# Left sides of seven-product matrix multiplication read from weights already split in DRAM, and the last product's rows apart

## The chip, the core and the metric

One Trainium2 chip, one of its NeuronCores. The metric is device time in microseconds for one execution of the whole program, shown as the median of several runs. Engines are called as in the profile: PE (TensorE), DVE (VectorE), ACT (ScalarE), POOL (GpSimd) and SP (SyncE, which issues all DMAs here).

## What is computed

A chunked attention gives 3072 rows of 512, and two feed-forward networks (FFN) follow, all in float32:

```python
x = attn_out.transpose(0, 2, 1, 3).reshape(B * S, H * D)   # 3072 x 512
h = np.maximum(x @ w_in, 0.0)                              # 512 x 2048
x = h * h @ w_out                                          # 2048 x 512
g = x @ w_gate                                             # 512 x 1536
silu = g * (1.0 / (1.0 + np.exp(-g)))
out = silu * (x @ w_val) @ w_out2                          # 1536 x 512
```

## The kernel before, in words

**Precision.** Each float32 operand is split into a high part (`hi`, ACT: a conversion, L445) and a low part (`lo`, DVE or POOL: operand minus hi, L452). A product is three matmuls: lo x hi, hi x lo, hi x hi (`TERMS`).

**Stages.** The rows come in six blocks of 512, in three pairs. Attention runs beside the first blocks. The first FFN of blocks 0 to 3 goes directly (`first_layer`, `first_out`), to about 446 us. What is left goes by pairs with a recursion of seven products in place of eight (Winograd's form of Strassen's): the second FFN of pairs 0, 1 and 2, and the first FFN of pair 2. TensorE then runs `second_quads` and `out_layer` for pair 0 (446 to about 632 us), for pair 1 (to about 797), `first_quads` and `out_layer` for pair 2's first FFN, and its second FFN (to 1128.7).

**Left and right sides.** Each of the seven products has a left side, made from four quarters of a weight, and a right side, made from the pair's data. `sides` makes the left ones: `ax` and `ay` are two tiles of 512 columns, each half of which is a quarter. Its `part` splits a result into hi and lo in one of four slots: slot 0 is `ax` as it is (products 1 and 2), slot 1 is a sum (5), slot 2 what two differences leave in `ax` (6 and 3), slot 3 a difference (7) and the second half of `ay` as it is (4). They are written to DRAM (`keep_in`, `keep_out`) and read back for the product (`load_in`, `load_out`). There are 18 calls of `sides` for the second FFN's weights (`left2`, DRAM names `tma`, `tmb`) and 16 for the first's (`left1`, `tla`, `tlb`). The first FFN's weights were split for the direct stage already; `keep1` writes these hi and lo to DRAM (`w1d`, names `win` and `wout`) in two rounds of the direct stage, and for `left1` `whole_of` reads hi and lo back and adds them (L883), so that `sides` can work on whole weights. Right sides are made by `rights` (sums and differences L464, then splits).

**Evictions.** When a product is done in its PSUM bank, ACT copies it (products 1, 5, 6 in `second_quads`; L473) or DVE combines it (3, 2, 7, 4; L464); then TensorE may write the bank again.

**Order.** Nothing of the order is written by hand. The kernel first lists operations with estimated costs, due times (`SIDES`: `left1`'s sides are due from 560 every 16 of its time units) and buffers; `Plan.run` plays through them and fixes each engine's order, buffers, and which engine takes an operation that may go on two (a split's low part, a quarter-wide sum: DVE or POOL; relu-square: ACT or DVE). So a removed operation can move everything behind it. PE may take an operation out of turn, up to 8 ahead, if one before it isn't ready (`ahead=8`). The engines follow the order and wait by semaphores.

**The end.** In the last `out_layer` product 4 adds six groups into two banks (`bank[i][0]`, `bank[i][1]`, rows of the result), six matmuls a group; then both are copied and written out.

## Time and profile before

| | |
|---|---|
| time, median of 3 runs | 1133.24 us (1132.12 to 1135.54) |
| the profiled execution, its own time | 1134.11 us |
| its span (first to last instruction) | 1132.4 us |
| mean granted TensorE clock | 0.997 of full speed |
| PE busy | 97% |
| DVE / ACT / POOL busy | 79% / 54% / 18% |
| DMA moved | 322.02 MB, mean 284 GB/s |

A row of the profile names the line of the kernel, the engine, the operation and the tiles (out<-in, buffer numbers left out): `ps` is a PSUM bank, `r`, `x`, `xx` and `w` hold split operands, `u`, `a` and `t` data tiles, `f`, `ff`, `g`, `gg` the tiles of the sides. "Idle before" is the time in which the engine stood still ahead of the instruction, and the releaser is what ended it. A busy PE isn't PE at its peak, since the profile models matmul ends.

### The profile page before, as it was taken

To read this page: it belongs to the slowest core of one execution; us is meant where nothing else is said; L and a number is where in the kernel's file an instruction comes from. 1 tells how busy PE (TensorE), PEld (TensorE's weight loads), DVE (VectorE), ACT (ScalarE), POOL (GpSimd) and SP (SyncE) were. 2 spreads that over 40 slices of the span, in tenths; PEclk is the share of its full clock that TensorE was granted. 3 is DMA by queue.
4 is the path that set the end of the run, shared out by engine and by line. 5 is a ranking of instruction groups with operands and counts; after the bars stand their busy time and mean duration, and the time that the engine had idled before them with its cause. 6 is when DMAs were issued, how large, how long until landed. Compare 5 with 4: busy or idle time off the path is not lost.

```text
span 1132.4 us, 17301 instructions
## 1 busy us (share of the span) xinstructions
PE 1097.3 (97%) x6044; PEld 893.7 (79%) x6044; DVE 891.4 (79%) x1576; ACT 611.8 (54%) x1077; POOL 200.6 (18%) x157
## 2 busy tenths in 40 slices
PE   5899999999999999999999999989999999999998
PEld 4677788888788887888788788868888887888886
DVE  6999889868888998678999866899867864534981
ACT  3878745454456566555664444555657642433550
POOL 2231011312112343000613300335101000000000
PEclk9999999999999999999999999999999999999999
DMA  8756667878888878999799999989996677765562
GB/s 335 242 201 214 217 232 276 286 274 313 286 313 273 279 265 319 407 326 348 238 351 369 406 413 385 358 319 373 370 379 222 194 236 289 237 196 177 180 183 93
DMA packets 118503, 322.02 MB, mean 284 GB/s; under 512 B 12816, under 2 KB 25104, under 8 KB 118416
## 3 DMA queue, kind: packets, MB, share of 16 engines
q1 hardware_dynamic: 118416, 320.92, 79.8%
q8 instruction: 48, 0.79, 0.3%
q14 instruction: 39, 0.32, 0.1%
HBM read 227.02 MB, written 93.85 MB: 283 GB/s over the span
## 4 chain that ended last, share of the span: by engine, by line
PE 80%; DVE 9%; DMA 5%; ACT 3%; issue 2%; POOL 1%; SPq 0%; DVEq 0%; ACTq 0%; POOLq 0%
PE ps L942 34%; PE ps L1077 18%; PE ps L712 13%; PE ps L740 12%; PE ps L519 2%; PE ps L646 2%; DVE r L452 2%; DVE f L425 1%; DVE f L433 1%; DVE f L410 1%; DMA s<-in_k 1%; ACT r L445 1%; DMA tla<-g 1%; DMA u<-yd 1%; DVE u L464 1%
## 5 line engine op out<-in xcount | busy, mean ns | idle before, releaser
L942 PE MATMUL ps<-r,r 128*128 128x512 f32 x1353 | 325.3, 392 | 8.8 <-DVE a L464 4.5
L942 PEld LDWEIGHTS ps<-r,r 128*128 128x128 f32 x1353 | 254.8, 189 | 64.5 <-DVE a L464 5.0
L473 ACT ACTIVATE t<-ps 128x512 f32<-128x512 f32 x172 | 101.4, 594 | 191.3 <-PE ps L942 79.3
L1077 PE MATMUL ps<-r,r 128*128 128x512 f32 x774 | 182.5, 390 | 0.1
L1077 PEld LDWEIGHTS ps<-r,r 128*128 128x128 f32 x774 | 145.4, 188 | 30.8 <-DVE f L464 0.7
L740 PE MATMUL ps<-r,w 128*128 128x512 f32 x564 | 138.6, 396 | 2.8 <-DVE w L452 2.7
L740 PEld LDWEIGHTS ps<-r,w 128*128 128x128 f32 x564 | 105.3, 188 | 28.0 <-DVE w L452 4.7
L445 ACT ACTIVATE r<-u 128x512 fp32r<-128x512 f32 x144 | 85.6, 624 | 40.3 <-PE ps L1077 16.6
L452 DVE TENSOR_TENSOR r<-u,r 128x512 fp32r<-128x512 f32 x130 | 90.7, 716 | 17.0 <-ACT r L445 12.4
L712 PE MATMUL ps<-xx,r 128*128 128x512 f32 x384 | 96.9, 401 | 3.0 <-DVE r L452 2.5
L712 PE MATMUL ps<-x,r 128*128 128x512 f32 x384 | 94.3, 394 | 0.0
L712 PEld LDWEIGHTS ps<-xx,r 128*128 128x128 f32 x384 | 70.6, 188 | 22.2 <-DVE r L452 5.1
L464 DVE TENSOR_TENSOR t<-t,ps 128x512 f32<-128x512 f32 x72 | 49.1, 685 | 43.5 <-PE ps L942 39.7
L712 PEld LDWEIGHTS ps<-x,r 128*128 128x128 f32 x384 | 70.9, 188 | 15.4
L595 DVE STREAM_TRANSPOSE a<-t 32x128 f32<-32x128 f32 x256 | 77.4, 302 | 4.5 <-PE ps L646 0.2
L473 ACT ACTIVATE t<-t 128x512 f32<-128x512 f32 x72 | 45.5, 632 | 63.0 <-DVE t L464 60.3
L445 ACT ACTIVATE r<-a 128x512 fp32r<-128x512 f32 x63 | 39.1, 626 | 53.0 <-PE ps L1077 27.1
L452 POOL TENSOR_TENSOR r<-t,r 128x512 fp32r<-128x512 f32 x30 | 45.7, 1522 | 109.3 <-ACT r L445 91.2
L942 PE MATMUL ps<-x,r 128*128 128x512 f32 x231 | 62.3, 391 | 0.2 <-DVE x L452 0.2
L942 PE MATMUL ps<-r,x 128*128 128x512 f32 x243 | 61.0, 392 | 0.0
L452 POOL TENSOR_TENSOR r<-u,r 128x512 fp32r<-128x512 f32 x14 | 21.4, 1528 | 222.6 <-ACT r L445 222.6
L445 ACT ACTIVATE g<-f 128x512 fp32r<-128x512 f32 (+1 forms) x75 | 42.8, 574 | 25.1 <-DVE f L433 8.8
(155 smaller groups left out, 1666.8 us busy)
## 6 DMA issues: line engine op xcount, KB each, us to landing
r<-tma SPq DMA_DIRECT2D x91, 512.0 KB, 6.5
g<-in_w SPq DMA_DIRECT2D x52, 512.0 KB, 4.7
r<-tmb SPq DMA_DIRECT2D x50, 512.0 KB, 5.8
tma<-g SPq DMA_DIRECT2D x29, 512.0 KB, 5.1
r<-tlb SPq DMA_DIRECT2D x24, 512.0 KB, 4.2
r<-tla SPq DMA_DIRECT2D x23, 512.0 KB, 7.0
a<-in_q SPq DMA_DIRECT2D x20, 512.0 KB, 5.8
a<-in_k SPq DMA_DIRECT2D x20, 512.0 KB, 5.6
```

Source lines behind the costliest of these rows:

```text
L410: lambda: nc.vector.tensor_scalar(out=at(a), in0=at(a), scalar1=EXP_MIN, scalar2=EXP_MAX, op0=ALU.max, op1=ALU.min),
L445: lambda: nc.scalar.activation(out=dst(HI), in_=src(), func=AF.Copy),
L452: eng.tensor_tensor(out=dst(LO), in0=src(), in1=dst(HI).bitcast(F32), op=ALU.subtract)
L464: eng.tensor_tensor(out=out[1](), in0=x[1](), in1=y[1](), op=op)
L473: nc.scalar.activation(out=out[1](), in_=x[1](), func=func)
L519: nc.tensor.matmul(o[64 * par : 64 * par + 64, s, f, m, :], q[:, s, m, ci, :], k[:, s, m, ci, :], start=True, stop=True,)
L595: nc.vector.transpose(out=o[g : g + 32, hh, :, :, m, :].rearrange("k s (f c) q -> k s f c q", c=2)[:, :, :, par, :], in_=a[r : r + 32, :, ...
L646: nc.tensor.matmul(o[64 * hh : 64 * hh + 64, 2 * s : 2 * s + 2, CH * ci : CH * ci + CH], a[:, hh, s, ci, :], b[:, hh, s, ci].rearrange("p ...
L712: nc.tensor.matmul(at(hp), at(w)[:, 512 * a + k * P : 512 * a + (k + 1) * P], x[:, b, k, :], start=(n == 0), stop=(n == len(terms) - 1),)
L740: nc.tensor.matmul(at(accs[m]), at(w)[:, 512 * a + m * P : 512 * a + (m + 1) * P], at(h2)[:, 512 * b : 512 * b + 512], start=(i == 0 and n ...
L942: nc.tensor.matmul(at(bank), at(w[slot])[:, o : o + P], at(r[i, n])[:, 512 * b : 512 * b + 512], start=(first and n == 0 and m == 0), stop ...
L1077: nc.tensor.matmul(at(bank[i][n]), at(w[i][g // 2])[:, o : o + P], at(r)[:, 512 * b : 512 * b + 512], start=(first and m == 0), stop=(g == ...
```

## The change

The direct stage's `keep1` writes each weight tile in two pieces, so that hi and lo of one quarter lie side by side, in runs of 1 KB: the layout that a left side has. For `left1` slot 0 and the second half of slot 3 are no longer split nor written by `sides`; products 1, 2 and 4 read `w1d` (slot 3 and products 1, 2, 4 of the output weights in two pieces instead of one). `whole_of` follows the layout, and its loads get 3 units more in the planner. In the last `out_layer` product 4 is listed by rows of the result: all groups for the first bank, then all for the second.

```diff
     def keep1(kind, i, j):
...
-        pl.op(
-            {"SP": 0.08},
-            lambda: nc.sync.dma_start(out=w1d[kind, i], in_=at(b).bitcast(F32)),
-            (b, (begun, (j, i))), (w1k[kind, i],), move=rate(524288),
-        )
+        for u in range(2):
+            pl.op(
+                {"SP": 0.08},
+                lambda u=u: nc.sync.dma_start(
+                    out=w1d[kind, i][:, 512 * u : 512 * u + 512].rearrange("p (h c) -> p h c", h=2),
+                    in_=at(b).bitcast(F32).rearrange("p (h u c) -> p u h c", u=2, h=2)[:, u],
+                ),
+                (b, (begun, (j, i))), ((w1k[kind, i], u),), move=rate(262144),
+            )
...
-    def sides(x, y, store):
+    def sides(x, y, store, given=False):
...
-        part(0, ax, 0, reads=((ax, 0), (ax, 1)))
+        if not given:
+            part(0, ax, 0, reads=((ax, 0), (ax, 1)))
...
-        part(3, ay, 0, reads=((ay, 0), (ay, 1)))
+        if given:
+            part(3, ay, 0, 256, reads=((ay, 0),))
+        else:
+            part(3, ay, 0, reads=((ay, 0), (ay, 1)))
...
         def load_in(self, q):
...
+                if self.given and n in (0, 3):
+                    d, key = self.given["in", 2 * q + n // 3]
+                    half = (512, 512, d[:, 512:1024], key)
+                    first = (0, 512, self.d_in[q][n][:, :512], (self.b_in[q], n))
+                    parts = [(0, 1024, d, key)] if n == 0 else [first, half]
...
         def keep_out(self, g, x, y):
...
-                    if slot == n:
+                    if slot == n and not (self.given and i in (1, 2, 4)):
...
         def load_out(self, i):
...
+                if self.given and i in (1, 2, 4):
+                    parts = []
+                    for m in range(2):
+                        d, key = self.given["out", 4 * n + 2 * m + (i > 1)]
+                        c = 512 * (i == 4)
+                        parts.append((512 * m, 512, d[:, c : c + 512], (key,)))
...
     def whole_of(parts):
...
-                for b, c in ((a, src), (t, 512 + src)):
+                k = wide // 256
+                for m, b in enumerate((a, t)):
...
-                            out=at(b)[:, o : o + wide], in_=w1d[key][:, c : c + wide]
+                            out=at(b)[:, o : o + wide].rearrange("p (u c) -> p u c", u=k),
+                            in_=w1d[key].rearrange("p (u h c) -> p u h c", u=2, h=2)[
+                                :, u : u + k, m, :
+                            ],
...
-                        (w1k[key], token), ((b, n),), move=rate(512 * wide),
+                        (w1k[key], token), ((b, n),), move=rate(512 * wide), tail=3.0,
...
     def out_layer(left, us, put, end=False):
...
+            if end and i == 4:
+                held[g] = r
+                if g < ng - 1:
+                    continue
+                for n in range(2):
+                    for h, r in held.items():
+                        pl.op(
+                            {"PE": 0.6875},
+                            lambda h=h, r=r, n=n: run(i, h, r, False, (n,)),
+                            (w[i][h // 2], r), (bank[i][n],), tail=0.2,
+                        )
+            else:
+                pl.op({"PE": 1.375}, run, (w[i][g // 2], r), bank[i], tail=0.2)
...
-    left1, left2 = Left("tl", NF1 // 2, NF1 // 2), Left("tm", NF2, NF2 // 2)
+    left1 = Left("tl", NF1 // 2, NF1 // 2, {k: (w1d[k], w1k[k]) for k in w1d})
+    left2 = Left("tm", NF2, NF2 // 2)
...
-        out_layer(left2, us, put_out(p))
+        out_layer(left2, us, put_out(p), end=p == NPAIR - 1)
```

The planner's order changes with it. Three places follow, before and after; a name's first number is its buffer or bank (`r22` is buffer 22 of the split operands), the one behind `_` counts tiles.

**PE, end of the program.** Products 2 (`ps2`, `ps5` before) and 7, and the start of 4, in the last `out_layer`; `x3` are the three matmuls of one group and bank. Before:

```order
L1077 MATMUL ps2_113<-r9_72,r14_77 128x512 x3
L1077 MATMUL ps5_116<-r9_72,r14_77 128x512 x3
L1077 MATMUL ps3_114<-r13_76,r19_82 128x512 x3
L1077 MATMUL ps7_118<-r13_76,r19_82 128x512 x3
L1077 MATMUL ps3_114<-r10_73,r15_78 128x512 x3
L1077 MATMUL ps7_118<-r10_73,r15_78 128x512 x3
L1077 MATMUL ps3_114<-r5_68,r15_78 128x512 x3
L1077 MATMUL ps7_118<-r5_68,r15_78 128x512 x3
```

The change:

```order
L1110 MATMUL ps1_112<-r4_67,r10_73 128x512 x3
L1110 MATMUL ps3_114<-r4_67,r10_73 128x512 x3
L1110 MATMUL ps4_115<-r19_82,r21_84 128x512 x3
L1110 MATMUL ps6_117<-r19_82,r21_84 128x512 x3
L1110 MATMUL ps4_115<-x0_86,r2_65 128x512 x3
L1110 MATMUL ps6_117<-x0_86,r2_65 128x512 x3
L1110 MATMUL ps4_115<-r11_74,r2_65 128x512 x3
L1110 MATMUL ps6_117<-r11_74,r2_65 128x512 x3
```

The banks have other numbers; the two banks of product 4 still take turns, three matmuls each, to the last row.

**POOL, then DVE, around the end of the first `second_quads` (before: 546 to 558 us).** POOL before, then in the change:

```order
L452 TENSOR_TENSOR r11_74<-u14_4304,r11_74 128x512
L883 TENSOR_TENSOR f2_96<-f2_96,f3_97 128x512
L464 TENSOR_TENSOR u14_4304<-u11_4301,u14_4304 128x512
L452 TENSOR_TENSOR r22_85<-u18_4308,r22_85 128x512
L464 TENSOR_TENSOR f5_99<-f0_94,f5_99 128x256
```

```order
L452 TENSOR_TENSOR r11_74<-u14_4336,r11_74 128x512
L464 TENSOR_TENSOR u7_4329<-u9_4331,u7_4329 128x512
L464 TENSOR_TENSOR u14_4336<-u11_4333,u14_4336 128x512
L452 TENSOR_TENSOR gg0_3342<-f0_94,gg0_3342 128x2x256
L464 TENSOR_TENSOR f0_94<-f0_94 128x256
```

The sum L883 is gone from here, and so are the split of `r22` and a quarter-wide sum. DVE over the same stretch, before and in the change:

```order
L433 ISA f0_94<-f0_94,f1_95 128x1024
L464 TENSOR_TENSOR t1_101<-t1_101,ps4_115 128x512
L464 TENSOR_TENSOR t2_102<-t2_102,ps7_118 128x512
L433 ISA f5_99<-f5_99,ff0_3306 128x1024
L464 TENSOR_TENSOR u19_4309<-ps3_114,u19_4309 128x512
L464 TENSOR_TENSOR ff2_3308<-f5_99 128x256
L464 TENSOR_TENSOR u19_4309<-u19_4309,t3_103 128x512
L452 TENSOR_TENSOR g0_87<-f0_94,g0_87 128x2x256
L452 TENSOR_TENSOR gg1_3311<-ff2_3308,gg1_3311 128x256
L464 TENSOR_TENSOR f0_94<-ff2_3308,f0_94 128x256
L452 TENSOR_TENSOR r6_69<-u2_4292,r6_69 128x512
```

```order
L433 ISA f0_94<-f0_94,f1_95 128x1024
L464 TENSOR_TENSOR t1_101<-t1_101,ps4_115 128x512
L464 TENSOR_TENSOR t2_102<-t2_102,ps7_118 128x512
L433 ISA f5_99<-f5_99,ff0_3338 128x1024
L464 TENSOR_TENSOR u19_4341<-ps3_114,u19_4341 128x512
L464 TENSOR_TENSOR ff2_3340<-f5_99 128x256
L464 TENSOR_TENSOR u19_4341<-u19_4341,t3_103 128x512
L464 TENSOR_TENSOR f5_99<-f0_94,f5_99 128x256
L452 TENSOR_TENSOR g0_87<-ff2_3340,g0_87 128x256
L464 TENSOR_TENSOR f0_94<-ff2_3340,f0_94 128x256
L452 TENSOR_TENSOR r22_85<-u18_4340,r22_85 128x512
```

Up to the eviction `u19<-ps3` and two rows behind it both are alike; behind them the split of `r22` stands on DVE.

**DVE, around the end of the second `second_quads` (before: 732 to 744 us).** Evictions read `ps`; rows of `f`, `ff`, `g` and `gg` belong to sides, the others to right sides. Before, then in the change:

```order
L452 TENSOR_TENSOR gg1_3311<-f2_96,gg1_3311 128x256
L452 TENSOR_TENSOR r3_66<-u15_4305,r3_66 128x512
L464 TENSOR_TENSOR u1_4291<-u20_4310,u1_4291 128x512
L464 TENSOR_TENSOR u15_4305<-u7_4297,u15_4305 128x512
L452 TENSOR_TENSOR g2_89<-f4_98,g2_89 128x2x256
L464 TENSOR_TENSOR a3_93<-ps1_112,t4_104 128x512
L452 TENSOR_TENSOR g1_88<-f5_99,g1_88 128x2x256
L464 TENSOR_TENSOR t2_102<-t2_102,ps6_117 128x512
L883 TENSOR_TENSOR ff0_3306<-ff0_3306,f0_94 128x512
L464 TENSOR_TENSOR t3_103<-t3_103,ps2_113 128x512
L464 TENSOR_TENSOR f4_98<-ff0_3306 128x256
L464 TENSOR_TENSOR a3_93<-ps4_115,a3_93 128x512
```

```order
L464 TENSOR_TENSOR a1_91<-a1_91,t3_103 128x512
L464 TENSOR_TENSOR u11_4333<-u21_4343,u11_4333 128x512
L452 TENSOR_TENSOR r4_67<-u4_4326,r4_67 128x512
L914 TENSOR_TENSOR f0_94<-f0_94,f2_96 128x512
L464 TENSOR_TENSOR a3_93<-ps1_112,t0_100 128x512
L452 TENSOR_TENSOR x0_86<-u8_4330,x0_86 128x512
L452 TENSOR_TENSOR r19_82<-u22_4344,r19_82 128x512
L464 TENSOR_TENSOR t1_101<-t1_101,ps2_113 128x512
L452 TENSOR_TENSOR r8_71<-u1_4323,r8_71 128x512
L464 TENSOR_TENSOR t2_102<-t2_102,ps3_114 128x512
L452 TENSOR_TENSOR r13_76<-a3_93,r13_76 128x512
L464 TENSOR_TENSOR a3_93<-ps4_115,a3_93 128x512
```

Rows of sides have given way to splits and sums of right sides; the eviction `a3<-ps4,a3` ends both pieces.

## Rows read from the trace of the kernel before

**Rows 1.** Busy time, share of the span and instructions, from the page.
```profile
PE 1097.3 (97%) x6044; PEld 893.7 (79%) x6044; DVE 891.4 (79%) x1576; ACT 611.8 (54%) x1077; POOL 200.6 (18%) x157
```

**Rows 2.** Waits of PE, 400 to 1133 us: total us, times, longest us.
```profile
PE ps L942 <- DVE a L464: 4.5, 1, 4.5
PE ps L942 <- DVE u L464: 3.7, 3, 2.0
PE ps L740 <- ACT x L445: 1.6, 1, 1.6
```

**Rows 3.** Timeline of PE at three places: start us, us, instructions [idle before <-releaser].
```profile
544.10 9.68 PE L942 MATMUL ps<-r,r 128*128 128x512 f32 x42
555.80 2.80 PE L942 MATMUL ps<-r,r 128*128 128x512 f32 x6 [2.02 <-DVE u L464]
...
637.20 3.00 PE L942 MATMUL ps<-r,r 128*128 128x512 f32 x12 [1.37 <-DVE u L464]
...
744.25 2.93 PE L942 MATMUL ps<-r,r 128*128 128x512 f32 x6 [4.54 <-DVE a L464]
```

**Rows 4.** Windows: us, busy per engine (instructions), PEclk, DMA share, GB/s.
```profile
550.00:560.00 10.00, 7.97 (x28) 6.12 (x27) 10.00 (x15) 5.79 (x12) 5.28 (x5) 0.83 0.49 155
...
630.00:640.00 10.00, 8.63 (x38) 6.86 (x37) 10.00 (x12) 5.63 (x10) 7.67 (x7) 1.00 1.04 405
...
670.00:680.00 10.00, 10.00 (x45) 8.26 (x45) 7.39 (x13) 4.92 (x9) 0.00 (x0) 1.00 1.03 417
...
740.00:750.00 10.00, 5.75 (x19) 4.67 (x20) 9.06 (x15) 5.32 (x10) 2.81 (x3) 0.83 0.85 266
...
560.00:637.00 77.00, 75.52 (x332) 61.90 (x330) 75.83 (x109) 42.76 (x77) 25.36 (x19) 1.00 0.98 365
```

**Rows 5.** Timeline of POOL and DVE before the first gap, 547 to 556 us.
```profile
547.91 1.74 POOL L883 TENSOR_TENSOR f<-f,f 128x512 f32<-128x512 f32 x1
549.62 1.48 POOL L464 TENSOR_TENSOR u<-u,u 128x512 f32<-128x512 f32 x1
551.06 1.75 POOL L452 TENSOR_TENSOR r<-u,r 128x512 fp32r<-128x512 f32 x1
...
551.57 1.78 DVE L433 CUSTOM_DVE_ANT_0 f<-f,f 128x1024 uint16<-128x1024 uint16 x1
...
555.07 0.68 DVE L464 TENSOR_TENSOR u<-ps,u 128x512 f32<-128x512 f32 x1
```

**Rows 6.** Timeline of DVE and POOL before the third gap, 730 to 744 us.
```profile
730.52 0.68 DVE L464 TENSOR_TENSOR a<-ps,a 128x512 f32<-128x512 f32 x1
...
734.60 3.49 DVE L464 TENSOR_TENSOR u<-u,u 128x512 f32<-128x512 f32 x2
...
735.79 1.75 POOL L883 TENSOR_TENSOR f<-f,ff 128x512 f32<-128x512 f32 x1
...
743.52 0.68 DVE L464 TENSOR_TENSOR a<-ps,a 128x512 f32<-128x512 f32 x1
```

**Rows 7.** Splits by form, 560 to 850 (third row 650 to 700): busy us, mean ns | idle.
```profile
L445 ACT ACTIVATE g<-f 128x512 fp32r<-128x512 f32 x23 | 14.4, 626 | 4.8 <-DVE f L464 2.0 <-POOL f L464 1.9 <-ACT r L445 0.6
...
L452 DVE TENSOR_TENSOR g<-f,g 128x512 fp32r<-128x512 f32 x23 | 20.4, 886 | 3.6 <-ACT g L445 3.5
...
L452 DVE TENSOR_TENSOR g<-f,g 128x256 fp32r<-128x256 f32 x2 | 0.8, 419 | 0.0
```

**Rows 8.** Window 130 to 330; DMA issues of the page: KB each, us to landing.
```profile
130.00:330.00 200.00, 200.00 (x1481) 162.02 (x1478) 166.04 (x381) 102.47 (x180) 37.18 (x35) 1.00 0.81 280
...
win<-r SPq DMA_DIRECT2D x16, 512.0 KB, 6.7
...
f<-wout SPq DMA_DIRECT2D x38, 128.0 KB, 4.8
```

**Rows 9.** Timeline at the end: the copies of the last two banks.
```profile
1128.01 0.60 ACT L473 ACTIVATE t<-ps 128x512 f32<-128x512 f32 x1 [23.56 <-PE ps L1077]
...
1128.69 0.69 DVE L471 COPY t<-ps 128x512 f32<-128x512 f32 x1 [7.91 <-PE ps L1077]
```

More of the change, by code (lines that the diff above doesn't have):

```diff
@@ L815, in store @@
             def store(n, w):
-                wide = 512 if n == 1 else 1024
+                wide = 512 if n == 1 or n == 3 and self.given else 1024
                 pl.op(
@@ L828, in load_in @@
                 wide = 512 if n == 1 else 1024
-                pl.op(
-                    {"SP": 0.08},
-                    lambda n=n, wide=wide: nc.sync.dma_start(
-                        out=at(w[n])[:, :wide].bitcast(F32), in_=self.d_in[q][n][:, :wide]
-                    ),
-                    ((self.b_in[q], n),), (w[n],), move=rate(512 * wide),
-                )
+                parts = [(0, wide, self.d_in[q][n][:, :wide], (self.b_in[q], n))]
+                if self.given and n in (0, 3):
[3 more added lines that the diff above has]
+                    parts = [(0, 1024, d, key)] if n == 0 else [first, half]
+                for o, wide, src, key in parts:
+                    pl.op(
+                        {"SP": 0.08},
+                        lambda n=n, o=o, wide=wide, src=src: nc.sync.dma_start(
+                            out=at(w[n])[:, o : o + wide].bitcast(F32), in_=src
+                        ),
+                        (key,), ((w[n], o),), move=rate(512 * wide),
+                    )
+                w[n].parts.setdefault(0, [None, []])
             return w
@@ L854, in load_out @@
             for n, b in enumerate(w):
-                pl.op(
-                    {"SP": 0.08},
-                    lambda n=n, b=b: nc.sync.dma_start(
-                        out=at(b).bitcast(F32),
-                        in_=self.d_out[i][:, 2 * n : 2 * n + 2, :].rearrange("p g c -> p (g c)"),
-                    ),
-                    ((self.b_out[i], 2 * n), (self.b_out[i], 2 * n + 1)), (b,), move=rate(524288),
-                )
+                parts = [
+                    (0, 1024, self.d_out[i][:, 2 * n : 2 * n + 2, :].rearrange("p g c -> p (g c)"),
+                     ((self.b_out[i], 2 * n), (self.b_out[i], 2 * n + 1)))
+                ]
+                if self.given and i in (1, 2, 4):
[4 more added lines that the diff above has]
+                        parts.append((512 * m, 512, d[:, c : c + 512], (key,)))
+                for o, wide, src, keys in parts:
+                    pl.op(
+                        {"SP": 0.08},
+                        lambda b=b, o=o, wide=wide, src=src: nc.sync.dma_start(
+                            out=at(b)[:, o : o + wide].bitcast(F32), in_=src
+                        ),
+                        keys, ((b, o),), move=rate(512 * wide),
+                    )
             return w
@@ L1052, in second_quads, with out_layer @@
         return got
-    def out_layer(left, us, put):
+    def out_layer(left, us, put, end=False):
         ng = len(us)
@@ L1071, in out_layer, with run @@
             first = g == 0 and i in (1, 5, 2)
-            def run(i=i, g=g, r=r, first=first):
-                for n in range(2):
+            def run(i=i, g=g, r=r, first=first, rows=range(2)):
+                for n in rows:
                     for m, (a, b) in enumerate(TERMS):
@@ L1082, in run @@
                         )
-            pl.op({"PE": 1.375}, run, (w[i][g // 2], r), bank[i], tail=0.2)
+            if end and i == 4:
[4 more added lines that the diff above has]
+                    for h, r in held.items():
+                        pl.op(
+                            {"PE": 0.6875},
+                            lambda h=h, r=r, n=n: run(i, h, r, False, (n,)),
+                            (w[i][h // 2], r), (bank[i][n],), tail=0.2,
+                        )
+            else:
+                pl.op({"PE": 1.375}, run, (w[i][g // 2], r), bank[i], tail=0.2)
             if g < ng - 1:
```

11 lines of the change are left out of this document (6 added, 5 removed).

## The prediction

> **What bounds the kernel now.** I read the page's busy shares first, then TensorE's waits, the timeline around each wait, a table of 10 us windows, and VectorE (DVE) against GpSimd (POOL) in those windows. TensorE is busy 97% of the span, and its work is not changed: the order lists as many TensorE instructions of each kind after as before. So the change can be worth only what TensorE loses. [rows 1]
>
> After the first 440 us it loses little [rows 2]: 1.6 us at the end of the direct stage, and 4.5 + 3.7 us on "DVE a L464" and "DVE u L464", evictions of PSUM banks in the product stages. In the timeline [rows 3] the three large ones are 2.02 us at 555.80, 1.37 us at 637.20 and 4.54 us at 744.25 (the fourth, 0.3 us at 566, is the rest of the 3.7). After two of them the matmuls are slow as well: 2.80 us for six at 555.80, where 42 took 9.68 us before it (0.23 us each, 1.4 for six). The windows [rows 4] show the clock: mean 0.83 in 550 to 560 and in 740 to 750, that is part of the time at 1.2 GHz instead of 2.4, 0.17 of 10 us or 1.7 us of work each. In 630 to 640, with the 1.37 us gap, it stayed at 1.00. Together 8.2 + 3.4 = 11.6 us is all that can come back from the product stages.
>
> Why is DVE late there? [rows 4]: in 550 to 560 and 630 to 640 it is busy 10.00 of 10 us, in all of 560 to 637 75.83 of 77; in 670 to 680, where POOL is idle, 7.39. Beside POOL its instructions stretch [rows 5]: an eviction that reads PSUM takes 0.68 us, but the instruction of two SBUF operands at 551.57 takes 1.78 while POOL's split at 551.06 runs. [rows 6] shows two subtractions in 3.49 us (normally 1.4) beside POOL's sum at 735.79; the eviction at 743.52 releases TensorE. So the bound in these places is DVE, lengthened by POOL; DMA is full too (share 1.04 in 630 to 640), but no TensorE wait there is put down to it.
>
> **The change, part by part.**
>
> *Sides of the first FFN's weights (16 calls).* Each loses the 512-wide split of slot 0 and half of the split of slot 3. [rows 7]: an ACT 512-wide conversion is 0.63 us; the DVE subtraction behind it is 0.68 undisturbed, 0.89 in the mean of 560 to 850; the 256-wide one is 0.42. Per side DVE or POOL saves 0.68 + (0.68 - 0.42) = 0.94 us, ACT about 0.85: 15 us and 14 us in all, over some 270 us. Most of it is worth nothing, since between the bursts DVE waits for TensorE. It counts where DVE is full.
>
> *The planner's new order.* By the order rows, DVE loses 20 instructions and POOL gains 9; five relu-squares move from ACT to DVE, in the last pair, where DVE has room. Up to DVE row 708 (the eviction at 555.07) nothing differs on DVE. I cost three places.
>
> (a) To 555.8. In the order, POOL's row behind `r11` is now `u7` instead of the sum, and the split `r22` that ran beside the 1.78 us instruction has gone to DVE, behind the eviction. Without it that instruction should take 0.68, and the 0.2 us by which the sum [rows 5] outlasts such a subtraction falls away: the eviction comes 1.3 us sooner and the gap is 0.7 us, too short to cost the clock if the 1.37 us gap is a guide.
>
> (b) To 637.2. DVE is saturated, so what counts is its own length between the evictions at 555.07 and 636.38 (81.3 us). Counted from the order: before 107 instructions of 512 columns and 8 of 256, now 100 and 16. Back to back they start 0.61 and 0.36 us apart, so 68.2 against 66.8 us: 1.4 us less. The remaining 13 us were stretching by POOL, 26 instructions, half a microsecond each. POOL's 512-wide sum and two 512-wide splits just ahead of 637 become 256-wide ones; between 0 and 3 us of gain, I take 0.5, since many 256-wide ones follow. Against it, in the new order TensorE comes to the waiting bank three matmuls (0.7 us) sooner. So at 637 TensorE is ahead by 1.3 + 1.4 + 0.5 - 0.7 = 2.5 us. That is less than what (a) alone hands over (1.3 + 1.7 of clock): TensorE arrives earlier and waits at 637 instead. Bounds: 5.4 (all it lost by then: 3.7 + 1.7), and 2.4 the other way (DVE gains nothing, the 0.7 is lost, and a gap of over 2 us there costs the clock's 1.7).
>
> (c) At 744. Between the two evictions at 730.52 and 743.52 DVE had 11 instructions of 512 and 3 of 256 columns, in the change 13 of 512 (third pair of order fences): the same 7.9 us. Beside it POOL ran six 512-wide instructions; in the change I count three and some four narrow ones: 3 x 1.0 (from the 3.49 us) - 4 x 0.4 (under the mean of (b)) = 1.4 us less stretching, and 0.4 us from a less late start. The 4.54 us become about 2.7, and the clock's 1.7 stays. Gain 1.8; bounds 6.2 (gap and clock), and 1 the other way (POOL's narrow ones gathering here).
>
> *keep1.* 32 writes of 512 KB become 64 of 256 KB with 1 KB runs. SP issues 32 more instructions of about 0.43 us; it waits for engines there, so nothing. TensorE has no gap in 130 to 330 [rows 8], and the DMA share is 0.81. A write lands after 6.7 us; the only other transfers with 1 KB runs, 128 KB of `wout`, land after 4.8 [rows 8]. Bounds for a pair: 6.7 us, and 4 x 4.8 = 19 us if everything scaled with bytes. I take the near end, because landing is mostly waiting in line, and cost it at nothing; the cover is the free 0.19 of DMA time.
>
> The Trainium skill's page "DMA: Bandwidth & Descriptors", section "Anatomy of one DMA", speaks against this edit: it fits a transfer as about 2.0 us fixed plus bytes at 436 GB/s, an estimate of 3.2 us for one of 512 KB and 5.2 us for two halves. By that the writes would take 1.6 times as long, which the free share would still hold.
>
> *Traffic from 560 to 850.* Eight stores of 768 KB and 24 of 256 KB go, 12.6 MB of 322; loads are the same bytes in 20 more pieces. No wait of TensorE hangs on DMA there, so zero, though DMA is full.
>
> *The last product by rows.* The order rows of TensorE's end say that it does not happen: the two banks still take turns, three matmuls each, as before. The planner gives the second row's step while the first row's next step waits for its accumulation. Only the last copy moves, from DVE to ACT [rows 9]: 0.60 for 0.69 us, 0.1 us.
>
> **Sum**, against the profiled execution of 1134.11 us (span 1132.4 and 1.7 around it): 2.5 + 1.8 + 0.1 = 4.4 us less, 1129.7. It was 0.9 above the median of three, 1133.24; the same on the median gives **1128.8 us**. A measurement of this kernel can tell about 0.3% (3.4 us) from no change: below 1129.8 is faster, above 1136.6 slower.
>
> **The rivals.**
>
> *All gaps close (chance 0.14).* 15 us less on DVE would be enough if POOL's narrower instructions fell between the bursts. For it: the gaps sit only where POOL is busy. Against: POOL has more instructions. 1133.2 - 11.6 - 0.1 = 1121.5.
>
> *DVE stays the bound and nothing is gained (0.32).* TensorE arrives sooner and waits longer at 637 and 744; with a gap of over 2 us at 637 the clock's 1.7 us moves there. For it: DVE waited for almost nothing in 560 to 637, and its new row there is only 2% shorter. (b) and (c) between a small gain and their lower ends: 1130 to 1136.6, about 1133.
>
> *Slower: the 1 KB runs (0.14).* keep1's 16.8 MB are 30% of the 56 MB moved in 130 to 330 (280 GB/s, [rows 8]), so 30% of 162 us of DMA time, 49 us. If 1 KB runs cost over 1.8 times as much, the free 38 us are gone; loads of the weights for the second FFN then land late, DVE and ACT stand behind them in order, and TensorE's evictions behind those. At 2 times it would be 10 us too much; half of it through DVE to TensorE gives 1133 + 5 = 1138. For it: bursts at full share stand there now. Against: the free share, and that TensorE has no gap at all there [rows 8].
>
> **How the numbers follow.** My forecast, gains of 3.4 to 8 us, has 0.40: around 1128.8, own range 1125 to 1130. With the closing of all gaps that makes 0.54 faster. The second rival is 0.32 for the same, the third 0.14 for slower. The range 1122.5 to 1135.0 leaves out most of the slower case and the edge of the fastest.
>
> **What would show it.** Right: DVE about 15 us less busy and ACT about 20; 12.6 MB less traffic; TensorE as busy, with the gap near 555 under 1 us at clock 1.00, one of 1 to 3 us near 635, one of 2 to 3 near 740; the two last banks still taking turns at the end. (b) is wrong if the gap near 635 is gone or if DVE waits for TensorE in 560 to 637. (c) is wrong if 740 to 750 has clock 1.00. A TensorE gap in 130 to 440 that was not there before, or writes of `win` landing after 10 us and more, would bring the third rival. The whole is wrong if new gaps appear behind 750, where I expect none.

## The result, and the profile after

| | before | the change |
|---|---|---|
| time, median of 4 runs each | 1133.23 us (1132.12 to 1135.54) | 1123.86 us (1122.14 to 1124.89) |
| ratio to before, 95% interval | | 0.9913 [0.9897, 0.9929] |
| the profiled execution, its span | 1134.11, 1132.4 us | 1124.73, 1123.0 us |

The change is 9.4 us faster, twice what I had forecast (4.4). The page after, in the lines that answer to [rows 1] (busy time, share and instructions of each engine; then the DMA's packets and what was written):

```profile
PE 1092.2 (97%) x6044; PEld 891.0 (79%) x6044; DVE 867.6 (77%) x1556; ACT 595.6 (53%) x1051; POOL 197.9 (18%) x166
...
DMA packets 133670, 309.43 MB, mean 276 GB/s; under 512 B 13136, under 2 KB 50000, under 8 KB 133584
...
HBM read 227.02 MB, written 81.26 MB: 275 GB/s over the span
```

The same 6044 matmuls; DVE is 23.8 us less busy (15 forecast), ACT 16.2 (20 forecast), and 12.6 MB are gone. DVE lost more than the 15 us of removed work. Two executions of before alone differ by 4.4 us in this (891.4 here, 887.0 in experiment 1); the rest would be steps that went to POOL (9 instructions more there) and stretching that went, which these rows don't tell apart. The waits of TensorE from 400 us on, to lay beside [rows 2] (total us, times, longest us):

```profile
PE ps L973 <- DVE u L464: 1.7, 1, 1.7
PE ps L973 <- DVE a L464: 1.6, 1, 1.6
PE ps L973 <- ACT r L445: 1.4, 1, 1.4
```

The timeline of TensorE at its gaps, to lay beside [rows 3] (start us, us, instructions, idle before):

```profile
543.83 6.96 PE L973 MATMUL ps<-r,r 128*128 128x512 f32 x30
552.53 1.65 PE L973 MATMUL ps<-r,r 128*128 128x512 f32 x6 [1.74 <-DVE u L464]
...
733.98 0.96 PE L973 MATMUL ps<-r,r 128*128 128x512 f32 x3 [1.60 <-DVE a L464]
...
945.13 0.50 PE L973 MATMUL ps<-r,x 128*128 128x512 f32 x1 [1.40 <-ACT r L445]
945.85 2.36 PE L973 MATMUL ps<-r,x 128*128 128x512 f32 x5 [0.22 <-DVE r L452]
```

The gap near 555 is hardly smaller (2.02 before), but the six matmuls behind it take 1.65 us, not 2.80, and the twelve behind those 2.88, not 3.37. The gap at 637 is gone. The one at 744 went from 4.54 to 1.60 us, and the matmuls behind it are not slow. A new gap stands at 945, with five slow matmuls behind it. The windows say the same of the clock (columns as in [rows 4]: PE, PEld, DVE, ACT, POOL, then clock and DMA share):

```profile
550.00:560.00 10.00, 8.26 (x37) 6.53 (x36) 10.00 (x17) 7.50 (x15) 6.79 (x4) 1.00 0.78 277
...
730.00:740.00 10.00, 8.40 (x37) 6.63 (x36) 10.00 (x14) 5.57 (x12) 6.47 (x6) 1.00 0.99 337
...
940.00:950.00 10.00, 8.38 (x29) 6.23 (x28) 6.26 (x11) 5.36 (x10) 0.00 (x0) 0.83 1.03 407
...
560.00:637.00 77.00, 77.00 (x342) 63.75 (x341) 72.65 (x118) 42.01 (x77) 19.30 (x17) 1.00 0.96 349
```

From 560 to 637 DVE does 118 instructions in 72.65 us, where 109 took 75.83 before [rows 4]: it has 4 us to spare, and TensorE loses nothing there.

Two profiles differ by more than the change, though. TensorE began the first product stage at 446.83 us before and at 443.89 now, where the order is the same but for the writes of keep1. So I read each profile in two pieces: S, where the first matmul of the product stages starts, and the time from there to the last matmul's end. That second piece was 681.8 us before and 675.4 now: 6.4 us of the 9.4 are in the product stages of this pair of profiles.

### The profile page after: what moved, and what is told of

Read it like the earlier page. It is cut to its first block, busy times and chain, and to the rows that moved or that the text cites. A ratio compares the mean times of both kernels' runs of the same rounds, so it can differ in the third digit from the quotient of the medians.

```text
span 1123.0 us, 17270 instructions
## 1 busy us (share of the span) xinstructions
PE 1092.2 (97%) x6044; PEld 891.0 (79%) x6044; DVE 867.6 (77%) x1556; ACT 595.6 (53%) x1051; POOL 197.9 (18%) x166
## 4 chain that ended last, share of the span: by engine, by line
PE 79%; DVE 11%; DMA 4%; ACT 3%; issue 2%; POOL 1%; SPq 0%; DVEq 0%; ACTq 0%; POOLq 0%
PE ps L973 34%; PE ps L1110 22%; PE ps L716 10%; PE ps L744 10%; PE ps L519 2%; DVE r L452 1%; DMA g<-in_w 1%; PE ps L646 1%; DVE f L425 1%; DVE a L595 1%; DVE f L433 1%; DVE f L410 1%; DMA s<-in_k 1%; DMA tlb<-gg 1%; ACT r L445 1%
## 5 line engine op out<-in xcount | busy, mean ns | idle before, releaser
L973 PE MATMUL ps<-r,r 128*128 128x512 f32 x1317 | 318.5, 390 | 3.6 <-DVE u L464 1.7
L973 PEld LDWEIGHTS ps<-r,r 128*128 128x128 f32 x1317 | 247.5, 188 | 56.5 <-DVE u L464 2.2
L1110 PE MATMUL ps<-r,r 128*128 128x512 f32 x786 | 187.4, 389 | 0.0
L1110 PEld LDWEIGHTS ps<-r,r 128*128 128x128 f32 x786 | 147.5, 188 | 30.7
L452 DVE TENSOR_TENSOR r<-u,r 128x512 fp32r<-128x512 f32 x136 | 96.8, 731 | 18.1 <-ACT r L445 12.4
L445 ACT ACTIVATE r<-u 128x512 fp32r<-128x512 f32 x145 | 86.7, 625 | 43.5 <-PE ps L1110 16.2
L716 PE MATMUL ps<-x,r 128*128 128x512 f32 x384 | 94.3, 394 | 0.0
L973 PE MATMUL ps<-x,r 128*128 128x512 f32 x315 | 85.8, 389 | 0.0
L716 PEld LDWEIGHTS ps<-x,r 128*128 128x128 f32 x384 | 70.9, 188 | 15.4
L973 PEld LDWEIGHTS ps<-x,r 128*128 128x128 f32 x315 | 59.1, 188 | 12.3
L445 ACT ACTIVATE r<-a 128x512 fp32r<-128x512 f32 x56 | 34.5, 626 | 46.3 <-DMA a<-yd 23.9
L973 PE MATMUL ps<-r,x 128*128 128x512 f32 x207 | 52.0, 395 | 1.6 <-ACT r L445 1.4
L744 PE MATMUL ps<-r,r 128*128 128x512 f32 x192 | 46.6, 391 | 1.5 <-DVE r L452 1.5
```

The source lines that it names most:

```text
L445: lambda: nc.scalar.activation(out=dst(HI), in_=src(), func=AF.Copy),
L452: eng.tensor_tensor(out=dst(LO), in0=src(), in1=dst(HI).bitcast(F32), op=ALU.subtract)
L716: nc.tensor.matmul(at(hp), at(w)[:, 512 * a + k * P : 512 * a + (k + 1) * P], x[:, b, k, :], start=(n == 0), stop=(n == len(terms) - 1),)
L744: nc.tensor.matmul(at(accs[m]), at(w)[:, 512 * a + m * P : 512 * a + (m + 1) * P], at(h2)[:, 512 * b : 512 * b + 512], start=(i == 0 and n ...
L973: nc.tensor.matmul(at(bank), at(w[slot])[:, o : o + P], at(r[i, n])[:, 512 * b : 512 * b + 512], start=(first and n == 0 and m == 0), stop ...
L1110: nc.tensor.matmul(at(bank[i][n]), at(w[i][g // 2])[:, o : o + P], at(r)[:, 512 * b : 512 * b + 512], start=(first and m == 0), stop=(g == ...
```

## The experiments

The theory: DVE, the engine behind the longest waits, is the bound of the product stages at a few places, POOL's instructions lengthen it, and the removed splits relieve it. The rivals: the planner's new order gains by itself; the 12.6 MB of traffic gain; the layout of keep1 does something to the direct stage; the 2.9 us ahead of 446 us are chance. All ratios are to the kernel before on the same chip.

**1. The kernel before once more.** No edit.

> The kernel before, once more, unchanged. In the changed kernel TensorE began the first product stage at 443.89 us, 2.9 us sooner than before (446.83), though the order of every engine up to there is the same but for the writes of keep1: 0.6 us of it stood there at 121 us, the other 2.4 came with a gap of 1.6 + 0.2 us at 443 that is gone. Theory 'chance': a second execution of the kernel before shows the same kind of spread there, 1 to 3 us, and its product stages start anywhere between 443.9 and 447. Rival 'layout': it starts at 446.8 within 0.5 us again, with the gap at 443, and so the 2.9 us belong to the change. Both expect the time within 0.2% of 1133.2 us, and the gaps near 555, 637 and 744 (2.0, 1.4, 4.5 us) again.

Measured: 1134.49 us, ratio 0.9996 [0.9984, 1.0009]; the profile's S is 443.42 us, with no gap at 443. So the start is chance. Over all 14 profiles of this study S lies between 443.4 and 445.6 in nine, and between 446.8 and 449.2 in five; just these five have a gap of 1.5 to 1.8 us at 443. Both kinds occur with the order of before and with that of the change. The piece behind S is 683.7 us here. And the clock told me something: two rows of this profile's TensorE.

```profile
552.38 1.65 PE L942 MATMUL ps<-r,r 128*128 128x512 f32 x6 [2.03 <-DVE u L464]
...
562.75 1.65 PE L942 MATMUL ps<-r,r 128*128 128x512 f32 x6 [1.91 <-DVE u L464]
```

The second one in the first profile of before:

```profile
566.16 1.65 PE L942 MATMUL ps<-r,r 128*128 128x512 f32 x6 [0.31 <-DVE u L464]
```

The same gap as in [rows 3], 2.03 us, but the clock didn't drop; and the gap 10 us later, 0.31 us before, is 1.91 here. Both times these six matmuls start 119.33 us behind S. What the clock doesn't take, the next eviction takes: DVE sets when that bank comes free. Experiment 2 has the same pair, 2.00 and 1.91 us at full clock. The gap of 4.5 us near 744 is here too (4.53); at 637 this execution waits twice for ACT instead, 0.78 and 1.22 us.

**2. The layout alone.** The order of before on all engines; keep1's one step issues two writes, and whole_of's loads follow.

```diff
+        def two():
+            for u in range(2):
+                nc.sync.dma_start(
+                    out=w1d[kind, i][:, 512 * u : 512 * u + 512].rearrange("p (h c) -> p h c", h=2),
+                    in_=at(b).bitcast(F32).rearrange("p (h u c) -> p u h c", u=2, h=2)[:, u],
+                )
```

> The kernel before with its own order on every engine; only keep1 writes in two pieces with 1 KB runs, and the loads of whole_of follow that layout. Theory of the prediction (runs of 1 KB cost nothing): 1133 us, within 0.3%, no TensorE gap in 130 to 330, first product stage at 446.8 or as far from it as the repeat of before. Rival 'slower by 1 KB runs': 1138 us, with new gaps in the direct stage. Rival 'the layout gains': the product stages start at 444 and the time is 1130.

Measured: 1134.67 us, ratio 1.0001 [0.9988, 1.0014]; one TensorE wait of 0.4 us between 130 and 440, and none between 130 and 330. The 1 KB runs cost nothing and gain nothing. A piece lands after 6.1 us, about as long as the whole did (6.7 us in [rows 8]); in the profile after:

```profile
win<-r SPq DMA_DIRECT2D x32, 256.0 KB, 6.0
```

The estimate in the prediction by the Trainium skill's page "DMA: Bandwidth & Descriptors", section "Anatomy of one DMA — SWDGE (gpsimd) path", was 5.2 us for two halves one behind the other. The section gives its fit for transfers issued by GpSimd, and all transfers here are issued by SyncE, so the estimate took it beyond what it is given for. No run here shows its 2.0 us of fixed cost as time on TensorE's path.

**3. The old order, the work left out.** The planner sees the lists of before; what the change removes is left out only when the instructions are written down, so every engine runs its old order with holes.

```diff
             split(dst, get, reads, ((w[n], 0),), n=wide, diff=POOLED)
+            if given and n == 0:
+                for o in pl.ops[first:]:
+                    o.fn = lambda e=None: None
```

(with `real = 256` for slot 3 and the stores and loads as in the change)

> The kernel before with its own order of all engines and its own choice of DVE or POOL for every step; what the change removes is left out where it stood: the 512-wide split of slot 0, the second half of the split of slot 3, and their stores; products 1, 2 and 4 of the first FFN read the weights as keep1 wrote them (new layout). The last product is as before. Theory 'removed work': the gaps near 637 and 744 shrink or go (DVE 12 to 15 us less busy), 1125 to 1129 us. Rival 'the planner's new order': without it next to nothing is gained, 1131 to 1134 us, and the gaps of 2.0, 1.4 and 4.5 us stay within 0.5 us each.

Measured: 1131.15 us, ratio 0.9964 [0.9951, 0.9977], a smaller gain than the theory's and a larger one than the rival's. DVE is 870.0 us busy, 21 less than before, the gap at 637 is gone, but TensorE's row near 744 reads

```profile
739.62 2.92 PE L984 MATMUL ps<-r,r 128*128 128x512 f32 x6 [3.53 <-DVE a L464]
```

with the 2.02 us near 555 as it was. The work alone is not the whole gain.

**4. The new order, the splits done all the same.** No stores come back.

```diff
+            real = 512 if given and n == 3 else wide
...
+            if given and n == 2:
+                hi, lo = pl.ops[first:]
+                hi.fn = lambda f=hi.fn: (f(), f())
+                lo.fn = lambda e, f=lo.fn: (f(e), f(e))
```

> The changed kernel with its own order, in which the removed split work is done all the same on the engine that does its neighbour: slot 3 is split over 512 columns instead of 256 and slot 2 is split twice (0.94 us more of DVE or POOL and about 0.85 of ACT in each of 16 sides); the stores stay left out. Theory 'removed work': a good part of the gain goes again, 1128 to 1132 us, with gaps of over 2 us near 552 to 556 or 734 to 745. Rival 'the planner's new order': 1124 to 1126 us. Rival 'less traffic': also 1124 to 1126, as the 12.6 MB are still gone.

Measured: 1130.58 us, ratio 0.9971 [0.9957, 0.9984]. That is the range that the theory gave, but part of the gain stays without the removed work. The gap near 555 is that of the change (1.74 us), so the splits play no part in it; the row near 734 has a gap between those of before and of the change:

```profile
733.92 1.16 PE L980 MATMUL ps<-r,r 128*128 128x512 f32 x3 [2.65 <-DVE a L464]
```

**5. The new order, the stores made all the same.** 768 KB a side more, from the tiles that are still made, to places that nothing reads.

```diff
+                    if self.given:
+                        spare = self.d_in[q][0][:, :512] if n == 1 else (
+                            self.d_in[q][0][:, 512:] if n == 2 else self.d_in[q][3][:, 512:]
+                        )
+                        nc.sync.dma_start(out=spare, in_=at(w)[:, :512])
```

(and one more store of 256 KB in each of three slots of `keep_out`)

> The changed kernel with its own order, in which the removed stores are made all the same: 16 times 768 KB more are written to DRAM, from the tiles of the slots that are still made, where nothing reads them (12.6 MB, 322 MB in all again). So far: with the old order and the work removed 0.36% are gained, with the new order and the splits kept 0.29%, and by the change 0.87%. Theory 'split work and order', each for about half: the stores cost nothing, 1123 to 1126 us, ratio 0.990 to 0.993. Rival 'traffic': the stores were the other half, 1127 to 1130 us (ratio 0.995 to 0.997), with TensorE or DVE waiting for loads between 560 and 850.

Measured: 1138.51 us, ratio 1.0029 [1.0015, 1.0044]: slower than before, and 1.2% worse than the change. The rival was right for this order, and by more than it said. TensorE's waits from 446 us on:

```profile
PE ps L985 <- ACT t L473: 3.8, 3, 2.9
PE ps L985 <- DVE a L464: 2.6, 1, 2.6
PE ps L985 <- ACT a L473: 2.4, 2, 2.1
PE ps L985 <- DVE u L464: 2.1, 2, 1.7
PE ps L1122 <- DMA r<-tmb: 2.3, 1, 2.3
```

Only 2.3 us are put down to a DMA. But the longest, 2.9 us at 705 behind an eviction by ACT, hangs on one too. ACT's timeline just ahead of that eviction:

```profile
703.95 0.42 ACT L445 ACTIVATE gg<-f 128x256 fp32r<-128x256 f32 x1 [4.83 <-DMA tla<-gg]
704.27 0.61 ACT L473 ACTIVATE t<-t 128x512 f32<-128x512 f32 x1
704.79 0.58 ACT L473 ACTIVATE t<-ps 128x512 f32<-128x512 f32 x1
```

A split waits 4.83 us for its buffer `gg`, which a store still reads; ACT follows its order, so the eviction `t<-ps` at 704.79, which TensorE waits for, stands behind it. A row of waits names only the last step of such a chain.

**6. The old order, only the stores left out.** Experiment 3 with the splits done.

```diff
-            real = 256 if given and n == 3 else wide
+            real = wide
-            if given and n == 0:
-                for o in pl.ops[first:]:
-                    o.fn = lambda e=None: None
```

> As the kernel with the old order and the removed work left out (ratio 0.9964 to before), but with the removed splits done as before: in the order of before only the stores of slot 0, of half of slot 3 and of products 1, 2 and 4 are left out, and the products read what keep1 wrote. Putting the stores back into the changed kernel cost 1.2%, putting the split work back 0.6%. Theory 'traffic': the stores are the larger part in the old order too, ratio 0.996 to 0.998 (1130 to 1132 us), with the gap at 637 gone. Rival 'split work': without the stores alone nothing is gained, 0.999 to 1.001, with the gaps of 2.0, 1.4 and 4.5 us as before. In the changed order the stores were then dear only because it was planned without them.

Measured: 1137.03 us, ratio 1.0022 [1.0008, 1.0035], gaps of 1.99 and 4.54 us as before, 0.84 at 638. With the order of before, leaving the stores out gains nothing. With the runs above this makes a table, all without the stores:

| | splits done | splits left out |
|---|---|---|
| order of before | 1.0022 (exp. 6) | 0.9964 (exp. 3) |
| new order | 0.9971 (exp. 4) | 0.9913 (the change) |

The splits are worth 0.58% in either order (1.0022 - 0.9964 and 0.9971 - 0.9913), 6.6 us of 1133; the new order is worth 0.51% in either case, 5.8 us. Each ratio is good to about 0.15%, so the two columns agreeing to the last digit is luck.

The two parts add up to 12.4 us, more than the 9.4 of the change, because experiment 6 itself came out 0.22% above before. Its profile starts late (S is 449.2 us), and behind S it is not longer than before: 682.1 us, against 681.8 and 683.7 in the two profiles of before. Read in this way, one profile each, the table is 682.1 and 679.6 us for the order of before, 679.9 and 675.4 for the new one. By it the splits are worth 2.5 or 4.5 us and the order 2.2 or 4.2. So both parts count, and each is worth somewhere between 2 and 7 us. Experiments 3 and 4 also run an order with work that it wasn't planned for; what an order loses by that may be part of their figures, and experiment 5 shows that it can be much.

**7. The new order without the 3 units for whole_of's loads.**

```diff
-                        (w1k[key], token), ((b, n),), move=rate(512 * wide), tail=3.0,
+                        (w1k[key], token), ((b, n),), move=rate(512 * wide),
```

> The changed kernel without the 3 units that the change gives the loads of whole_of in the planner: the same work and the same bytes, another order from about 560 us on. Theory 'the order's share was luck': the time is anywhere from 1121 to 1131 us, as the work is worth 4 us and the order what falls out. Rival 'what is removed fixes the time': 1123 to 1125 us whatever the order, and gaps of TensorE behind 446 us that sum to 4 to 6 us.

Measured: 1129.25 us, ratio 0.9945 [0.9927, 0.9963]. The same work in another order gives back a third of the gain, at a place of its own: a gap of 2.14 us at 614, behind an eviction by ACT. So, as far as two orders can show it, the order's share is not a property of the removed work; it is one draw of the planner.

**8. POOL out of the product stages.** On the changed kernel, planned anew.

```diff
+        if pl.alone:
+            costs = {"DVE": costs["DVE"]}
...
+    pl.alone = True
     for q in range(NF1 // 2):
         left1.keep_in(
```

(the same in `sub` and in the sum of `whole_of`)

> The changed kernel in which the sides of the first FFN and all right sides may use DVE alone: some 60 steps go from POOL to DVE, and POOL is idle behind about 560 us; the order is the planner's with that. Theory 'POOL stretches DVE by nearly what it takes off' (in 560 to 637 before, 26 POOL instructions took about 13 us of stretching, against 26 x 0.61 = 16 us had DVE done them): 1122 to 1130 us, DVE instructions of two SBUF operands at 0.68 us throughout. Rival 'POOL carries what DVE has no room for': DVE has no idle time in 540 to 570 and 710 to 740, about 20 more instructions there make TensorE wait 8 to 12 us more, 1132 to 1140 us.

Measured: 1120.04 us, ratio 0.9862 [0.9839, 0.9886], better than the change and better than the theory asked. The gaps near 555 and 734 are gone altogether; TensorE loses 2.5 us in all behind 446.

**9. The same order as the change, POOL's steps on DVE.** Nothing is planned anew.

```diff
+        if o.n >= first_side and o.eng == "POOL":
+            o.eng = "DVE"
         o.fn(o.eng) if o.fn
```

> The changed kernel with its own order of steps, in which each step of the product stages that the planner gave to POOL (67 rows) is issued to DVE instead, at the place that it has in the list. Nothing is planned anew. Theory 'what stretched is gone': DVE takes the steps at 0.61 us each without stretching, 1121 to 1126 us, as good as with POOL or better. Rival 'it was the new order that gained': in this order DVE meets the extra steps where it has no room, its evictions come late, 1127 to 1133 us; then the 1120.0 us of the kernel without POOL are the planner's order.

Measured: 1122.24 us, ratio 0.9900 [0.9885, 0.9915]: with 75 instructions more on DVE (the expectation had counted 67) not slower than the change. The piece behind S is 671.3 us, against 675.4 in the change and 674.1 in experiment 11, which has the change's order up to its last product. The windows (DVE is the third pair):

```profile
540.00:560.00 20.00, 20.00 (x90) 16.57 (x89) 20.00 (x38) 13.16 (x24) 2.43 (x2) 1.00 0.72 242
...
560.00:637.00 77.00, 77.00 (x342) 63.75 (x341) 73.25 (x135) 42.65 (x78) 0.00 (x0) 1.00 0.98 357
```

In 560 to 637 DVE does 135 instructions in 73.25 us, where the change did 118 in 72.65: POOL's 17 instructions were taken over for 0.6 us. In 540 to 560, where DVE has no idle time in either, the change has 26 instructions in 20.00 us (and POOL 10),

```profile
540.00:560.00 20.00, 18.26 (x81) 14.81 (x80) 20.00 (x26) 11.51 (x22) 14.89 (x10) 1.00 0.60 205
```

and this kernel 38, with no gap of TensorE. The gap near 734 is still there, 1.31 us.

**10. The kernel before without POOL in the product stages.** The edit of experiment 8 on the kernel before, nothing of the change.

> The kernel before, without any part of the change, whose sides of the first FFN and right sides may use DVE alone (the same edit as in the kernel of 1120.0 us). Theory 'POOL stretches DVE by what it takes off, and the planner orders better without it': a gain of the same size as on the changed kernel (0.5%), 1125 to 1130 us, and the gaps of 2.0 and 4.5 us at 555 and 744 under 1 us each. Rival 'only with the work removed has DVE room for it': with 15 us more of sides DVE is overfull, 1133 to 1140 us.

Measured: 1132.24 us, ratio 0.9980 [0.9967, 0.9994]: a gain too small for the theory, and no loss. The piece behind S is 682.3 us, no shorter than before. All the gaps of [rows 3] are gone, as the theory had it, and others have come, between 770 and 810. TensorE's waits from 446 us on:

```profile
PE ps L948 <- DMA r<-tla: 3.2, 1, 3.2
PE ps L1083 <- DVE r L455: 1.9, 3, 1.0
PE ps L1083 <- ACT r L446: 1.5, 1, 1.5
```

A left side of pair 2's first FFN is read 3.2 us late, at 809. That DVE alone makes the sides too late with the old work is argued from this row, not shown.

**11. The last product really by rows**, on the change, and **12.** on the kernel without POOL.

```diff
                 for n in range(2):
-                    for h, r in held.items():
...
+                    pl.op(
+                        {"PE": 0.6875 * len(held)},
+                        lambda n=n: [run(i, h, r, False, (n,)) for h, r in held.items()],
+                        [w[i][h // 2] for h in held] + list(held.values()), (bank[i][n],), tail=0.2,
+                    )
```

> The changed kernel in which product 4 of the last out_layer is listed as one step of 18 matmuls for each row of the result, so that the planner can't mix the two: the order now ends with 18 matmuls into one bank and then 18 into the other. Expected by the prediction's reading (only the last copies can gain): the first bank's copy and its write lie under the second bank's 4.1 us of matmuls, one copy of 0.6 us is left behind the last matmul, and the end comes 0.5 to 0.7 us sooner: no difference that the timing can show from the changed kernel (1123 to 1125). Rival 'the planner's order moves more than that': over 2 us either way, from some gap ahead of 1110.

> The kernel without POOL in the product stages (1120.0 us, ratio 0.9862), with the last product by rows as well (one step of 18 matmuls a row). Expected: the two gains add, 0.5 to 1.0 us less at the end: 1119 to 1120 us, ratio 0.984 to 0.988. If the planner's order moves other places, up to 3 us either way.

Measured: 1124.18 us, ratio 0.9899 [0.9875, 0.9923], and 1119.74 us, 0.9880 [0.9863, 0.9897]. Neither can be told from its kernel with mixed rows (0.9913 and 0.9862). The end of the change, ACT's last row, and that of experiment 11:

```profile
1118.66 1.28 ACT L473 ACTIVATE t<-ps 128x512 f32<-128x512 f32 x2 [23.55 <-PE ps L1110]
```

```profile
1114.35 0.60 ACT L473 ACTIVATE t<-ps 128x512 f32<-128x512 f32 x1 [21.38 <-PE ps L1110]
1118.43 0.60 ACT L473 ACTIVATE t<-ps 128x512 f32<-128x512 f32 x1 [3.48 <-PE ps L1110]
```

By rows, the first copy is done 4 us ahead of the end. But from the last matmul's end to the end of the span it is 3.7 us in both (1119.31 to 1123.0, and 1118.39 to 1122.1), as before the change (1128.66 to 1132.4): with mixed rows the first copy is already under way when the second bank gets its last matmuls.

Of these kernels, 4 and 5 do work that nothing uses. The two without POOL (8 and 12) beat both the kernel before, by 1.4 and 1.2%, and the change, by 0.5 and 0.3%.

## Why the prediction was right, and where its sizes were off

**Direction, mechanism and the wide range held** (1122.5 to 1135.0; 1123.86 measured). The forecast's own range, 1125 to 1130, was missed by 1.1 us, on the side of the rival "all gaps close" (1121.5). DVE in its full stretches, lengthened by POOL, was the bound: experiment 9 shows it for the gap near 555 without any change of order. The sum was half the gain, and each of its two large terms came out another way than I had worked it out.

**(a), near 555: wrong in both halves, the gap and the clock.** I let the gap fall from 2.02 to 0.7 us, because POOL's split beside the 1.78 us instruction was gone. It fell to 1.74. Another row of POOL had come in its place. DVE and POOL ahead of the eviction at 551.79, after:

```profile
544.92 3.18 POOL L464 TENSOR_TENSOR u<-u,u 128x512 f32<-128x512 f32 x2
...
550.04 1.28 POOL L452 TENSOR_TENSOR gg<-f,gg 128x512 fp32r<-128x512 f32 x1 [1.94 <-ACT gg L445]
...
546.87 0.68 DVE L464 TENSOR_TENSOR u<-ps,t 128x512 f32<-128x512 f32 x1
...
550.37 1.50 DVE L433 CUSTOM_DVE_ANT_0 f<-f,ff 128x1024 uint16<-128x1024 uint16 x1
551.79 0.68 DVE L464 TENSOR_TENSOR u<-ps,u 128x512 f32<-128x512 f32 x1
```

The `gg` split stands in the order rows of the change, and I gave it no price. The rows of experiment 9 in the same place, where POOL has two rows left in 540 to 560:

```profile
549.93 0.93 DVE L433 CUSTOM_DVE_ANT_0 f<-f,ff 128x1024 uint16<-128x1024 uint16 x1
550.79 0.68 DVE L464 TENSOR_TENSOR u<-ps,u 128x512 f32<-128x512 f32 x1
```

The eviction comes 1 us sooner, and this profile's S is 1.7 us later: 2.7 us more room, and the gap of 1.74 is gone. The clock's 1.7 us in this place (1.6 by the rows: 1.1 in the six matmuls, 0.5 in the twelve behind them) were no gain by themselves: a repeat of before without the drop lost as much 10 us later (experiment 1).

**(b), to 637: the mechanism right, the sign of the left-over wrong.** I said TensorE would arrive earlier and wait at 637 instead, and that the step is wrong if that gap is gone. It is gone, with the old order as well (experiment 3). The mis-sized term is the stretching, set at 0.5 us within bounds of 0 and 3: in 560 to 637 an instruction of DVE took 0.70 us in the mean before (75.83 / 109), 0.62 after (72.65 / 118) and 0.54 with POOL idle (73.25 / 135, experiment 9). Against that last, an estimate since the widths are not mixed alike, the stretching fell from some 16 to some 9 us.

**(c), at 744: right in kind, half the size.** I counted the same 7.9 us of DVE between two evictions of the stage's last products, and 1.4 us less stretching. After, the rows between the same two evictions are

```profile
723.08 0.68 DVE L464 TENSOR_TENSOR a<-ps,a 128x512 f32<-128x512 f32 x1
723.68 1.18 DVE L464 TENSOR_TENSOR u<-u,u 128x512 f32<-128x512 f32 x1
724.77 1.78 DVE L464 TENSOR_TENSOR a<-a,t 128x512 f32<-128x512 f32 x1
...
729.70 1.22 DVE L452 TENSOR_TENSOR r<-u,r 128x512 fp32r<-128x512 f32 x1
...
733.25 0.68 DVE L464 TENSOR_TENSOR a<-ps,a 128x512 f32<-128x512 f32 x1
```

10.17 us from eviction to eviction, against 13.00 in [rows 6] (730.52 to 743.52): 2.8 us less. Now 13 starts 0.60 us apart would make 7.8 us of it, so the stretching fell from about 5.1 to 2.4 us. I had counted three wide POOL instructions and priced the narrow ones at 0.4 us each; two wide ones stood there, beside which DVE lost 1.6 us, and beside the five narrow ones that began between 728.5 and 732.7 it lost 0.8. The clock's 1.3 us (six matmuls in 2.93 against 1.65) did come back here, which I had ruled out: 740 to 750 has clock 1.00 after, the sign that I had named for (c) being wrong.

**keep1 and the traffic: zero, as forecast, for the order that was planned with them.** Experiment 2 shows the first, experiment 6 the second. My reason for the second was too short: "no wait of TensorE hangs on DMA" is true of the rows, which name the last step only. Put the stores back into an order planned without them, and they cost 1.2%.

**The last product** kept its mixed rows, as the order rows said. I gave it 0.1 us; it is nothing, and done by rows it is nothing either.

**Behind 750** I expected no new gap, and named one as the sign that the whole is wrong. One came at 945 (1.40 + 0.22 us, and 2.36 for five matmuls), where before 0.22 + 0.30 us were lost behind 955. With the same order up to there, experiment 11 has 0.65 us and five in 1.42, so its size is chance, and it took back less than the places (a) to (c) gave. By the releasers it is a split that ACT could start only when TensorE was done with the stage before (2.63 us of ACT's waiting, to 943.77).

**The sum.** For the pair of profiles: 1.6 of clock and 0.3 at 555, 1.7 at 566 and 637, 2.9 and 1.3 at 744, less 2.3 at 945, is 5.5 of the 6.4 us behind S; the other 0.9 I can't place. The 3 us ahead of S are chance in this pair, and over many runs the ratio stands without them. Of the rivals, "nothing is gained" and "1 KB runs" fell; "all gaps close" was not far off, and without POOL it nearly holds (experiment 8: 2.5 us of gaps left).

**How far the cause is settled.** That the splits and the order both count is shown (the table in experiment 6); that each gives half is not. That the splits act through DVE's full stretches is shown by the gaps at 637 and near 734 in experiments 3 and 4. Why this order is better than that of before is not: ahead of 734 its rows of sides lie elsewhere, but experiment 7 is a near order too, and lost 3.6 us of it. And a gap that closes isn't a gain by itself: without POOL all three gaps of the kernel before close, and 0.2% is left of it (experiment 10). What was not tried is the order of the change with only one of these places altered.

## What to carry to other kernels

An engine whose instructions stretch another's is no free help: before giving it steps to relieve the other, count what the other loses in the same windows (here 17 steps taken back cost 0.6 us in 77, and the change without POOL is 1.2 to 1.4% under before; the kernel before without POOL only 0.2%). When removing work lets a planner order everything anew, run both crossings (old order with the work left out, new order with the work done): here each gave a part. Such a run has an order that was planned for other work, and may pay for that too. And compare two profiles from a common event on; 3 of the 9 us of this pair of profiles were chance ahead of the first of them.

## What the hardware showed that I had not expected

- POOL's share of the product stages was worth nothing to the time: nearly all its steps on DVE, in the same places, gave 0.9900 against 0.9913. The Trainium skill's page "SBUF — State Buffer", section "SBUF: two separate sides", calls the port pair that the two share an exclusive lock for a whole instruction, also for a DVE instruction with two SBUF operands against a POOL one that reads SBUF. The rows shown at (a) agree: 1.50 us beside POOL's split for two SBUF operands, and 0.68 beside POOL's sums for the instruction at 546.87, which reads PSUM.
- The same program has two starts of its product stages, 443.4 to 445.6 and 446.8 to 449.2 us.
- A gap of 2.03 us was followed by full clock in one execution and by slow matmuls in another of the same kernel (2.02 us); one of 1.40 us by slow ones at 945, those of 1.74 and 1.60 us by full clock, and one of 2.89 us in experiment 5 as well (at 705, then 21 matmuls in 5.05 us).
